# Retention attention with a SwiGLU block on one core: VectorE's operations on the shared port wait for GpSimd's, as GpSimd's already wait for VectorE's

## The chip, the cores and the metric

The kernel runs on one core of one Trainium2 chip, in one launch. The metric is the device time of that launch in microseconds (us); lower is better. The core's engines are TensorE (PE in the rows; PEld is its weight load), VectorE (DVE), ScalarE (ACT), GpSimd (POOL) and SyncE (SP, whose sequencer SPq issues nearly all DMAs). Each engine runs its own list of instructions in order, and instructions of different engines are ordered by semaphores alone.

## The reference

The input is q, k, v of shape (4, 8, 768, 64) in float32, a decay per head, and three weights of a gated layer with 512 inputs and 1536 hidden columns.

```python
for b in range(nb):                      # blocks of 64 tokens
    intra = einsum('bhic,bhjc->bhij', qb, kb) * Dmask
    intra = einsum('bhij,bhjd->bhid', intra, vb)
    inter = einsum('bhid,bhde->bhie', qb * lam_pow, kv_state)
    out[:, :, sl] = intra + inter
    kv_state = lam_block * kv_state + einsum('bhsd,bhse->bhde', kb * rev_pow, vb)
...                                      # x = out as 3072 tokens x 512
xn = x / sqrt(mean(x * x, -1) + 1e-6) * rms_g
g, val = xn @ w_gate, xn @ w_val
result = (g * sigmoid(g) * val) @ w_out  # float32
```

## The kernel before, in words

Tokens go in 6 groups of 512 (index `m`), heads in 4 pairs (`p`), hidden columns in 12 blocks of 128 (`f`). The work of all stages is interleaved:

- **Retention** for a group and a pair (class `Pair`): score products into PSUM tiles `pa`; VectorE multiplies them by the decay mask (`decay_a`, L497, tile `a`); ScalarE decays k (L487); GpSimd multiplies q by the powers in place (`decay_q`, L501, tile `qkv`); VectorE carries the state (L523, L525); TensorE sums in `po` (`mix_chunks` L538, `mix_states` L549, which reads the decayed q). ScalarE squares the result and GpSimd or VectorE adds the squares (`add_squares`, L578, tile `sq`).
- **Norm** (`first_norm_steps`, `norm_steps`, class `Norm`): the mean (L608), GpSimd's power -0.5 (`root`, L612, tile `y`), its rests (L619), the spread by TensorE (`pr`), the scaled rows `xn` (L636).
- **Float32 as two float16 parts**: every operand of a large product is split in a high part (ScalarE, a copy) and a low part, the difference (`low`: L440 for weights, L644 for x, L663 for the sums `tx`, L729 for the weights' sums `ws`, L922 and L1013 for the hidden rows, L290 for the output weights). VectorE or GpSimd makes the low parts.
- **Weights** (class `Weights`) are first decoded (L209 on ScalarE, `convert` L216 and L219 on VectorE), their squares summed (L416), a power of two chosen as scale (L426, L430) and undone later (`undo`, L445, tile `cg`).
- **Products**: in the first 24 units (one unit is a group and a block `f`) the gate and value products are done plainly (L668, tiles `pg` and `pv`). From then on they take seven half-size products instead of eight (`strassen`, L779, tiles `pa` and `pb`), with operand sums that GpSimd (`whole`, L708, tile `r`) and VectorE (`sums`, L717 to L721, tile `ws`) prepare; VectorE adds the partial products (L837, L845) and forms the hidden values (`mul_sums`, L857, tile `sg`), which SyncE stores (L873). SyncE also loads the prepared weights `gv` (L740) and `gw` (L745). The output product follows (L938, L1050).

**What sets the order.** All of this is recorded as steps, each with an engine, a cost, a due time and what it reads and writes. A planner (`Plan.run`) lays the steps on model clocks and returns one list; the kernel then issues its instructions in that order, so each engine's own list is fixed. The table `SHIFTS` moves due times.

**The shared port.** The planner treats all of GpSimd's steps, and those VectorE steps whose function stands in the set `SHARED`, as users of one port that only one of the two engines holds at a time (`Plan.shared`, L1150 to L1152):

```python
def shared(self, i):
    eng, fn = self.steps[i][0], self.steps[i][3]
    return eng == "POOL" or eng == "DVE" and fn.__name__ in self.SHARED
...
if self.shared(i):                     # in ready(): not before the other engine is through
    t = max(t, held["DVE" if eng == "POOL" else "POOL"] - 0.13)
```

So in the plan each of the two waits for the other. When the steps are issued (the loop at the end of the kernel, from L1961), a GpSimd step gets a real semaphore wait for the last shared VectorE operation that the plan puts ahead of it. A shared VectorE step gets no such wait for the GpSimd step ahead of it: it waits for its data alone. Nothing else in the program depends on this wait; it is there for the port.

In `SHARED` are, among others, `low`, `sums`, `mul_sums` (L857), `convert`, `add_squares`, `scale` (L426), `undo` (L445) and `rest` (L619).

Of the kernel before, what the change touches and what calls it, by code (L numbers as in the profile page):

```python
# [22 lines left out]
def retention_swiglu_kernel(  # L23
# [11 lines left out]
    nc = tc.nc  # L35
# [1463 lines left out]
    def arrive_steps():  # L1499
        def arrive():  # L1500
            pass

        step("LD", 4.3, -9, arrive, w=["cs", "come"])
        times = [0.75, 1.3, 1.55, 1.35, 1.85, 1.3, 1.3, 1.3]
        for p in range(NP):
            for i, c in enumerate(("qK", "kv")):
                step("LD", times[2 * p + i], -9, arrive, w=["come", *[f"q0_{p}:{x}" for x in c]])
        step("LD", 3.05, -9, arrive, w=["come", "gv0"])

    def ramp_steps():  # L1510
        pm = []

        def largest_of_all():
            pm.append(scales())

        def make_scales():
            scales_of(pm[0])

        step("DVE", 0.13, -3.1, largest, r=["cs"], w=["gmax"])
        step("PE", 0.3, -3.1, largest_of_all, r=["gmax"], w=["pmax"], new=[("pmax", "g")])  # L1520
        step("DVE", 1.33, -2.35, make_scales, r=["pmax"], w=["gs"])
        for p in range(NP):
            for part in range(3):
                w = f"pw{p}" if part == 2 else f"mask{2 * p + part}"
                step("DVE", 0.38, -3.2 + 0.4 * p + 0.15 * (part == 2), powers, p, part, r=["cs"] + ["wv11"] * (part == 2), w=[w])
        ats = [-2.85, -2.3, -2.0, -1.75]
        pairs = [Pair(0, p) for p in range(NP)]
        for q, at in zip(pairs, ats):
            pair_scores(q, at)
            pair_sums(q, at + 0.4)  # L1530
            pair_mix(q, at + 0.5)
        first_norm_steps(0, -0.3, 0.05)
        for p, at in enumerate(ATTENTION_1):
            q = Pair(1, p)
            pair_scores(q, at)
            pair_sums(q, at + 0.5)
            pair_mix(q, at + 0.6)
        first_norm_steps(1, 5.0, 0.05)
        for f, at in enumerate(CONVERT):
            wt = Weights(f)  # L1540
            if wt.halves:
                for i in range(2):
                    halved_steps(wt, at + 0.2 * i, i)
            else:
                convert_steps(wt, at)
                split_steps(wt, at + 0.35)
# [196 lines left out]
    def load_steps():  # L1743
        queue = [(1, 0), (1, 1), (1, 2), 1, (1, 3), *range(2, NF)]
        queue += [(m, p) for m in range(2, NG) for p in range(NP)]
        for n, key in enumerate(queue):
            cost = 2.65 if n < 5 else 3.0 if n < 10 else 3.6
            lasts = (0.1, 0.1, 0.5, 0.4)[n] if n < 4 else 2.3
            if isinstance(key, tuple):
                m, p = key  # L1750
                if key == (3, 1):
                    step("LD", 0.0, -9, operand_tiles, new=[("tx0", "in"), ("tx1", "in")],
                         w=[f"{t}:{o}{i}" for t in ("tx0", "tx1") for o in "hl" for i in range(2)]
                         + [f"vals{i}:{j}" for i in range(2) for j in range(2)])
                name = f"q{m}_{p}"
                step("LD", cost, -9, load_qkv, m, p, w=[f"{name}:{c}" for c in "qKkv"], new=[(name, "in")], lasts=lasts)
            else:
                step("LD", cost, -9, load_gv, key, w=[f"gv{key}"], new=[(f"gv{key}", "in")], lasts=lasts)
# [123 lines left out]
    with tc.manual_schedule(  # L1882
        engines={
            mybir.EngineType.PE, mybir.EngineType.DVE, mybir.EngineType.Activation,
            mybir.EngineType.Pool, mybir.EngineType.SP,
        }
    ):
        hs = {u: Hidden(u, m, f) for u, (m, f) in enumerate(units)}
        columns = {u: [] for u in range(2 * NF)}
        arrive_steps()  # L1890
        load_steps()
        ramp_steps()
        out_weights = [out_weight_steps(j, at) for j, at in enumerate(OUT_W)]
        end = len(units)
        pair = None
        for u in range(end):
            for f in COLUMNS.get(u, []):
                columns[u + 1].append(column_steps(f, u - 0.7))
            if u == FACTORS:
                factor_steps(u)  # L1900
            for f in range(NF):
                if int(SUMS[f]) == u:
                    sum_steps(f, SUMS[f])
            h = hs[u]
            m, f = h.m, h.f
            if u < 2 * NF:
                classical(u, h, columns[u])
                n = u - (2 * NF - 8)
                if 0 <= n < NP:
                    q = Pair(2, n)  # L1910
                    pair_scores(q, u + 0.62)
                    pair_sums(q, u + 0.64)
                    if pair:
                        pair_mix(pair, u + 0.63)
                    pair = q
                elif n == NP:
                    pair_mix(pair, u + 0.63)
                elif n == NP + 1:
                    norm_steps(2, u, 0.11)
                if u == 2 * NF - 1:  # L1920
                    pair = Pair(3, 0)
                    pair_scores(pair, u + 0.62)
            else:
                strassen(u, h)
                p = (f + 1) // 2 % HALF
                following = m + 2 if f == NF - 1 else m + 1
                if f % 2 == 0 and pair:
                    pair_sums(pair, u + 0.12)
                    pair_mix(pair, u + 0.3)
                    pair = None  # L1930
                if f % 2 and p < NP and following < NG:
                    pair = Pair(following, p)
                    pair_scores(pair, u + 0.1)
                if f == 2 * NP - 1 and m + 1 < NG:
                    norm_steps(m + 1, u, 0.2)
        if PLAIN:
            step("ROOM", 0.0, START[0] - 3, early_room, new=[("early", "big0")], w=["early:"])
        for m in range(PLAIN):
            for j in range(HALF):
                block_steps(m, j, START[m] - 1.5 - 0.3 * (HALF - 1 - j), 0.1)  # L1940
            plain_rows_steps(m, START[m], PLAIN_LENGTH)
        for o, at in zip(out_weights, OUT_SUMS):
            out_sum_steps(o, at)
        for i in range(2):
            room_step(i, START[PLAIN] - 3)
        for m, at in enumerate(START):
            if m < PLAIN:
                continue
            for j in range(HALF):
                t = at - AHEAD[j]  # L1950
                if m == NG - 1:
                    t = units.index((NG - 1, 2 * j + 1)) + 0.5
                operand_steps(m, j, t, 0.1)
            rows_steps(m, at, LENGTH)
        for i, by in SHIFTS.items():
            eng, cost, at, *rest = plan.steps[i]
            plan.steps[i] = (eng, cost, at + by, *rest)
        order = plan.run()
        now, gaps = 1.5, True
        traced, ahead = nc.cur_bb.bb.instructions, None  # L1960
        for t, i in order:  # L1961
            eng, cost, _, fn, args, _, _, new, _ = plan.steps[i]
            begun = len(traced)
            if eng == "PE":
                if any(name.startswith("pb") for name, _ in new):
                    gaps = False
                idle = t - now
                if gaps and idle > 0.8:
                    busy(int((idle - 0.5) / 0.24))
                now = t + cost  # L1970
            fn(*args)
            if plan.shared(i):

                engine = mybir.EngineType.Pool if eng == "POOL" else mybir.EngineType.DVE
                mine = [x for x in traced[begun:] if x.engine == engine]
                if eng == "DVE":
                    ahead = mine[-1].name
                elif ahead:
                    tc.add_manual_dep(
                        mine[0], ahead,  # L1980
                        mybir.DependencyInfo(mybir.DependencyClass.Sync, mybir.DependencyReason.DATA),
                        reason="shared port",
                    )
                    ahead = None

# [63 lines left out]
```

## Time and profile before

| | us |
|---|---|
| median of 3 runs (lowest, highest) | 629.96 (629.2, 631.78) |
| the profiled execution, its own time | 629.99 |
| its span, first to last instruction | 628.2 |
| busy: PE / PEld | 622.2 / 479.3 |
| busy: DVE / ACT / POOL | 452.8 / 383.9 / 127.6 |
| GpSimd instructions | 113 |
| VectorE instructions | 886 |

Busy time is the union of an engine's instructions. A matmul's end is modelled, so that a busy TensorE can still lose time between starts; and an operation that stands at a port counts as busy. In a row of the timeline, a number in brackets is the engine's idle time just before the instruction and what ended it. Granted clock is the share of TensorE's full 2.4 GHz; it was 1.000 over the whole span.

### The profile page before, as it was taken

How to read it: one execution, taken by the hardware profiler on the slowest of the kernel's cores; microseconds unless marked ns; L12 is line 12 of the kernel's file. 1: busy time of each engine (PE TensorE's matmuls, PEld its weight loads, DVE VectorE, ACT ScalarE, POOL GpSimd, SP SyncE). 2: the span in 40 equal slices, each digit the busy share in tenths (PEclk: the TensorE clock that was granted, in tenths of full speed). 3: DMA queues.
4: the chain of work that ended last, by engine and by line, in shares of the span. 5: the costliest groups of instructions: out<-in, count | busy, mean ns of one | idle time of the engine just before them, and what ended most of it. 6: DMA issues, size and time to landing. Idle time of an engine off the chain costs nothing.

```text
span 628.2 us, 14174 instructions
## 1 busy us (share of the span) xinstructions
PE 622.2 (99%) x5665; PEld 479.3 (76%) x5665; DVE 452.8 (72%) x886; ACT 383.9 (61%) x724; POOL 127.6 (20%) x113
## 2 busy tenths in 40 slices
PE   9999999999999999999999999999999999999997
PEld 8864444455657777668888888888889888888886
DVE  6889888777787778788875789634874778546641
ACT  3779799986546764568764685534853564445531
POOL 3531201142825665410020110011000110000000
DMA  8899898888646788878878667744675667343401
GB/s 320 305 318 299 313 313 290 288 279 290 231 148 226 258 284 273 275 265 284 269 268 297 216 212 225 244 179 152 226 224 179 202 207 248 109 135 105 148 18 51
DMA packets 56033, 144.05 MB, mean 229 GB/s; under 512 B 5920, under 2 KB 18208, under 8 KB 54560
## 3 DMA queue, kind: packets, MB, share of 16 engines
q1 hardware_dynamic: 55824, 142.64, 67.3%
q8 instruction: 44, 0.72, 0.5%
q10 hardware_dynamic: 144, 0.52, 0.3%
q14 instruction: 21, 0.17, 0.1%
HBM read 106.96 MB, written 36.18 MB: 228 GB/s over the span
## 4 chain that ended last, share of the span: by engine, by line
PE 94%; DMA 2%; DVE 1%; ACT 1%; SPq 0%; issue 0%; POOL 0%; ACTq 0%; POOLq 0%
PE o L1050 20%; PE pa L779 20%; PE pb L779 15%; PE pv L668 9%; PE pg L668 9%; PE o L938 5%; PE pa L477 4%; PE po L538 3%; PE po L549 3%; DMA qkv<-in_qkv_dram 2%; PE o_own L1050 2%; PE pst L510 2%; PE pss L589 1%; PE unread L144 1%; PE pr L630 0%
## 5 line engine op out<-in xcount | busy, mean ns | idle before, releaser
L779 PEld LDWEIGHTS <-gw 128*128 128x128 f16 x1440 | 139.5, 98 | 21.9 <-issue 0.8
L1050 PE MATMUL o<-wo,late 128*128 128x256 f16 x1152 | 143.9, 273 | 0.5 <-ACT late L1061 0.5
L1050 PEld LDWEIGHTS <-late 128*128 128x128 f16 x1260 | 123.0, 98 | 15.1 <-issue 0.8
L668 PEld LDWEIGHTS <-w_half 128*128 128x128 f16 x576 | 53.9, 98 | 60.5 <-issue 1.5
L833 ACT COPY tx<-pa 128x256 f32<-128x256 f32 x96 | 35.3, 371 | 72.9 <-PE pa L779 55.5
L779 PE MATMUL pa<-tx,gw 128*128 128x256 f16 x576 | 77.4, 273 | 0.0
L668 PE MATMUL pv<-x,w_half 128*128 128x512 f16 x288 | 69.2, 379 | 0.2
L668 PE MATMUL pg<-x,w_half 128*128 128x512 f16 x288 | 66.8, 379 | 0.0
L837 DVE TENSOR_TENSOR tx<-pb,tx 128x256 f32<-128x256 f32 x96 | 40.0, 420 | 31.4 <-PE pb L779 29.1
L779 PEld LDWEIGHTS <-gv 128*128 128x128 f16 x576 | 56.0, 98 | 7.4 <-issue 0.2
L501 POOL TENSOR_TENSOR qkv<-qkv,pw 128x512 f32<-128x512 f32 x24 | 30.6, 1275 | 74.8 <-PE pa L477 66.5
L845 DVE TENSOR_TENSOR sg<-pb,sg 128x256 f32<-128x256 f32 x48 | 20.1, 422 | 35.4 <-ACT sg L841 30.7
L1013 DVE TENSOR_TENSOR late<-s,late 128x1024 f16<-128x1024 f32 x30 | 37.3, 1253 | 5.2 <-ACT late L1009 5.1
L708 POOL TENSOR_TENSOR r<-w_half 128x512 f32<-128x512 f16 x24 | 27.7, 1163 | 63.3 <-DVE w_half L440 25.5
L497 DVE TENSOR_TENSOR a<-pa,mask 128x512 f32<-128x512 f32 x48 | 31.4, 683 | 12.0 <-PE pa L477 8.5
L779 PE MATMUL pa<-x,gv 128*128 128x256 f16 x288 | 39.3, 273 | 0.0
L779 PE MATMUL pb<-x,gv 128*128 128x256 f16 x288 | 39.3, 273 | 0.0
L779 PE MATMUL pa<-x,gw 128*128 128x256 f16 x288 | 39.0, 273 | 0.0
L779 PE MATMUL pb<-tx,gw 128*128 128x256 f16 x288 | 39.0, 273 | 0.0
L779 PE MATMUL pb<-x,gw 128*128 128x256 f16 x288 | 38.7, 273 | 0.0
L938 PE MATMUL o<-wo,early 128*128 128x512 f16 x144 | 34.9, 379 | 0.0
L729 POOL TENSOR_TENSOR ws<-ws,ws 128x512 f16<-128x512 f32 x24 | 28.8, 1210 | 29.3 <-DVE en L325 15.3
(152 smaller groups left out, 1031.0 us busy)
## 6 DMA issues: line engine op xcount, KB each, us to landing
gw<-gw_kept SPq DMA_DIRECT2D x48, 640.0 KB, 4.8
qkv<-in_qkv_dram SPq DMA_DIRECT2D x47, 512.0 KB, 6.0
h<-h_kept SPq DMA_DIRECT2D x30, 512.0 KB, 4.1
h_kept<-sg SPq DMA_DIRECT2D x48, 256.0 KB, 3.4
gv<-gw_kept SPq DMA_DIRECT2D x48, 256.0 KB, 4.4
raw_gv<-in_weights_dram SPq DMA_DIRECT2D x11, 1024.0 KB, 7.2
raw_o<-in_weights_dram SPq DMA_DIRECT2D x24, 256.0 KB, 4.4
gw_kept<-ws SPq DMA_DIRECT2D x12, 512.0 KB, 4.2
```

The costliest lines, as they stand in the source:

```text
L477: nc.tensor.matmul(self.pa[j][:, c, :], self.kT[r, c, :], self.qT[r, c, :], start=True, stop=True,)
L497: nc.vector.tensor_mul(self.a[:, j], self.pa[j], decay)
L501: eng.tensor_mul(self.qT, self.qT, pw[:, p : p + 1, :].broadcast_to([P, GC, P]))
L668: nc.tensor.matmul(ps, w[:, kk, :], x[:, kk, :], start=i == kk == 0, stop=i == 2 and kk == NK - 1,)
L708: nc.gpsimd.tensor_add(self.r[:, i], w[:, 0], w[:, 1])
L729: eng.tensor_sub(self.to[:, c, 1], self.t[:, c], self.to[:, c, 0])
L779: nc.tensor.matmul(ps, w(ow, k), x(ox, k), start=first and i == k == 0, stop=i == 2 and k == 1, skip_group_check=True,)
L833: nc.scalar.copy(self.val_sums[:, self.half(t)], self.pa)
L837: nc.vector.tensor_add(v, self.pb, v)
L938: nc.tensor.matmul(self.banks[t], h[:, oh, t * P : (t + 1) * P], wo[:, j, 3 + 2 * k : 5 + 2 * k, ow], start=j == k == i == 0, stop=j == HA ...
L1013: eng.tensor_sub(lo, of, hi)
L1050: nc.tensor.matmul(bank[:, t], ops[:, oh, t * P : (t + 1) * P], w[:, ow], start=n in (1, 2, 5) and q == i == 0 and (t == 0 or bank is own) ...
```

## The change

`ahead` held the last shared VectorE operation, and only a GpSimd step took it up as a wait. It becomes a table with an entry for each of the two engines: a shared step of either one takes up the other's latest entry, waits for it, and leaves its own. `mine[0]` is the first instruction of the step, which gets the wait, and `mine[-1]` the last, which is waited for.

```diff
-        traced, ahead = nc.cur_bb.bb.instructions, None
+        traced, ahead = nc.cur_bb.bb.instructions, {}
+        engines = {"POOL": mybir.EngineType.Pool, "DVE": mybir.EngineType.DVE}
         for t, i in order:
...
             fn(*args)
             if plan.shared(i):
 
-                engine = mybir.EngineType.Pool if eng == "POOL" else mybir.EngineType.DVE
-                mine = [x for x in traced[begun:] if x.engine == engine]
-                if eng == "DVE":
-                    ahead = mine[-1].name
-                elif ahead:
+                name = "POOL" if eng == "POOL" else "DVE"
+                mine = [x for x in traced[begun:] if x.engine == engines[name]]
+                other = ahead.pop("DVE" if name == "POOL" else "POOL", None)
+                if other:
                     tc.add_manual_dep(
-                        mine[0], ahead,
+                        mine[0], other,
                         mybir.DependencyInfo(mybir.DependencyClass.Sync, mybir.DependencyReason.DATA),
                         reason="shared port",
                     )
-                    ahead = None
+                ahead[name] = mine[-1].name
```

No instruction is added, removed or moved on any engine: all five lists hold the same rows in the same order. What changes is who waits. 63 VectorE instructions now wait for a GpSimd operation for which neither they nor an earlier instruction of VectorE waited before; older waits that a new one covers fall away. GpSimd's waits for VectorE stay as they were.

VectorE's list at the place where the sums of one weight block are made (`ws` from `r`), with the scores of a pair (`a`), the hidden values of a unit (`sg`) and a block of hidden rows (`early`) behind them. Semaphores stand in brackets: Pool is GpSimd's, DVE VectorE's own, Activation ScalarE's, DMAHW a DMA's.

```order
-L717 TENSOR_TENSOR ws_2717<-r_2585 128x256
+L717 TENSOR_TENSOR ws_2717<-r_2585 128x256 [waits Pool_49]
 L718 TENSOR_TENSOR ws_2717<-r_2585 128x256
-L720 TENSOR_TENSOR ws_2717<-r_2585,ws_2717 128x256 [waits DVE_49]
+L720 TENSOR_TENSOR ws_2717<-r_2585,ws_2717 128x256 [waits Pool_49]
 L721 TENSOR_TENSOR ws_2717<-r_2585,ws_2717 128x256 [waits DVE_49]
 L497 TENSOR_TENSOR a_2_2751<-pa_2_0_2730,mask 128x512 [waits DVE_49,PE_49]
 L497 TENSOR_TENSOR a_2_2751<-pa_2_1_2731,mask 128x512 [waits PE_49]
-L857 SCALAR_TENSOR_TENSOR sg_1_2636<-tx_2210,cg,sg_1_2636 128x512 [waits Activation_49]
+L857 SCALAR_TENSOR_TENSOR sg_1_2636<-tx_2210,cg,sg_1_2636 128x512 [waits Activation_49,Pool_49]
```

Three of these six steps now stand behind a GpSimd operation: the first sums behind the squares' addition, the second sums behind a `whole` (L708), the hidden values behind `decay_q` (L501). The order is as it was.

VectorE's list at the first halved weight block (f = 1), where the scale of one half is made (`e`, `sc`) and the low part of the other is formed (`w_half`):

```order
 L219 SCALAR_TENSOR_TENSOR w_1_553<-raw_gv_509,w_1_553 128x512 [waits DVE_49]
-L426 TENSOR_SCALAR e_1_697<-pn_0_674 128x1 [waits PE_49]
+L426 TENSOR_SCALAR e_1_697<-pn_0_674 128x1 [waits PE_49,Pool_49]
 L430 TENSOR_SCALAR sc_698<-e_1_697 128x1 [waits DVE_49]
 L497 TENSOR_TENSOR a_3_708<-pa_3_0_685,mask 128x512 [waits PE_49]
 L497 TENSOR_TENSOR a_3_708<-pa_3_1_686,mask 128x512 [waits PE_49]
-L440 SCALAR_TENSOR_TENSOR w_half_95<-w_0_552,sc_698,w_half_95 128x512 [waits Activation_49]
+L440 SCALAR_TENSOR_TENSOR w_half_95<-w_0_552,sc_698,w_half_95 128x512 [waits Activation_49,Pool_49]
```

Here L426 stands behind an addition of squares on GpSimd (L578), which itself waits for the L219 just ahead of L426, and L440 behind a `decay_q` (L501).

## Rows read from the trace of the kernel before

**Rows 1.** The page: the span, and each engine's busy time with its share of the span and its instructions.

```profile
span 628.2 us, 14174 instructions
PE 622.2 (99%) x5665; PEld 479.3 (76%) x5665; DVE 452.8 (72%) x886; ACT 383.9 (61%) x724; POOL 127.6 (20%) x113
```

**Rows 2.** All of TensorE's waits that the trace lists: who waited for whom, us in total, how often, the longest.

```profile
PE unread L144 <- POOL ident masks.py:199: 1.5, 1, 1.5
PE pss L589 <- POOL sq L578: 0.5, 1, 0.5
PE o L1050 <- ACT late L1061: 0.5, 1, 0.5
```

**Rows 3.** A stretch of the span in which GpSimd works most: its length, then busy us (and instructions) of PE, PEld, DVE, ACT and POOL, the granted clock, the DMAs' share, GB/s.

```profile
200.00:240.00 40.00, 40.00 (x411) 30.96 (x409) 30.71 (x58) 25.06 (x49) 25.25 (x22) 1.00 0.83 275
```

**Rows 4.** Timeline, VectorE and GpSimd at single places: start us, us, engine, line, operation, out<-in, shapes. First an L857 with GpSimd idle, then a GpSimd operation and the VectorE operation that waits for it.

```profile
246.34 0.75 DVE L857 SCALAR_TENSOR_TENSOR sg<-tx,cg,sg 128x512 f32<-128x512 f32 x1
...
247.17 1.16 POOL L708 TENSOR_TENSOR r<-w_half 128x512 f32<-128x512 f16 x1 [0.92 <-DVE sg L857]
...
248.36 0.42 DVE L717 TENSOR_TENSOR ws<-r 128x256 f32<-128x256 f32 x1 [0.28 <-POOL r L708]
```

**Rows 5.** Timeline at 232 us: VectorE, then GpSimd, then TensorE.

```profile
232.14 1.66 DVE L857 SCALAR_TENSOR_TENSOR sg<-tx,cg,sg 128x512 f32<-128x512 f32 x1
...
234.06 2.06 DVE L922 TENSOR_TENSOR early<-h,early 128x1024 f16<-128x1024 f32 x1
236.04 0.41 DVE L837 TENSOR_TENSOR tx<-pb,tx 128x256 f32<-128x256 f32 x1
...
232.11 1.15 POOL L708 TENSOR_TENSOR r<-w_half 128x512 f32<-128x512 f16 x1
233.88 1.15 POOL L708 TENSOR_TENSOR r<-w_half 128x512 f32<-128x512 f16 x1 [0.63 <-DVE sg L857]
...
236.51 0.38 PE L779 MATMUL pb<-tx,gw 128*128 128x256 f16 x2
```

**Rows 6.** Timeline at 211 to 217 us: VectorE, then GpSimd, then TensorE's weight loads.

```profile
211.78 1.11 DVE L717 TENSOR_TENSOR ws<-r 128x256 f32<-128x256 f32 x1
...
213.25 0.42 DVE L720 TENSOR_TENSOR ws<-r,ws 128x256 f32<-128x256 f32 x1
213.71 1.26 DVE L721 TENSOR_TENSOR ws<-r,ws 128x256 f32<-128x256 f32 x1
...
211.34 1.27 POOL L578 TENSOR_TENSOR sq<-sq,sq 128x512 f32<-128x512 f32 x1 [3.45 <-DVE ws L721]
213.37 1.32 POOL L708 TENSOR_TENSOR r<-w_half 128x512 f32<-128x512 f16 x1 [0.76 <-DVE ws L718]
215.05 1.15 POOL L708 TENSOR_TENSOR r<-w_half 128x512 f32<-128x512 f16 x1 [0.36 <-DVE ws L721]
216.16 1.27 POOL L501 TENSOR_TENSOR qkv<-qkv,pw 128x512 f32<-128x512 f32 x1
...
217.49 0.19 PEld L549 LDWEIGHTS po<-qkv,state 64*64 64x64 f32 x4 [0.23 <-POOL qkv L501]
```

**Rows 7.** Timeline at 40 to 43 us: VectorE, GpSimd, ScalarE, TensorE's weight load and matmuls.

```profile
40.57 0.15 DVE L426 TENSOR_SCALAR e<-pn 128x1 int32<-128x1 int32 x1
...
40.82 1.27 POOL L578 TENSOR_TENSOR sq<-sq,sq 128x512 f32<-128x512 f32 x1 [4.38 <-DVE e L426]
...
41.95 0.71 ACT L436 ACTIVATE w_half<-w,sc 128x512 f16<-128x512 f32 x1
...
42.77 0.31 PEld L668 LDWEIGHTS <-w_half 128*128 128x128 f16 x2
...
42.34 1.02 PE L668 MATMUL pg<-x,w_half 128*128 128x512 f16 x4
```

**Rows 8.** Timeline at 60 to 65 us: VectorE, GpSimd, ScalarE, TensorE.

```profile
60.15 0.22 DVE L445 TENSOR_SCALAR cg<-e,cx 128x2 int32<-128x2 int32 x1
61.09 0.69 DVE L216 TENSOR_SCALAR w<-w 128x1024 int32<-128x1024 int32 x1 [0.72 <-ACT w L209]
...
60.32 1.50 POOL L612 TENSOR_TENSOR y<-ms,power 128x4 f32<-128x4 f32 x1 [11.38 <-DVE sc L430]
...
63.15 0.63 ACT L416 ACTIVATE junk<-w 128x512 bf16<-128x512 f32 x1 [0.29 <-DVE w L219]
...
64.44 0.18 ACT L416 ACTIVATION_READ_ACCUMULATOR junk<-w 128x1 f32 x1
...
64.68 0.16 PE L420 MATMUL pn<-ssq,ones_b 128*128 128x2 bf16 x1
```

**Rows 9.** Timeline, VectorE and GpSimd at 28 us and at 264 us.

```profile
28.56 0.73 DVE L440 SCALAR_TENSOR_TENSOR w_half<-w,sc,w_half 128x512 f16<-128x512 f32 x1
28.11 1.03 POOL L612 TENSOR_TENSOR y<-ms,power 128x4 f32<-128x4 f32 x1 [0.62 <-DVE w_half L440]
...
263.81 0.42 DVE L274 TENSOR_TENSOR t<-wo_again,t 128x256 f32<-128x256 f32 x1
264.27 1.74 DVE L275 TENSOR_TENSOR t<-wo_again,t 128x256 f32<-128x256 f32 x1
264.04 1.69 POOL L663 TENSOR_TENSOR tx<-xt,tx 128x768 f16<-128x768 f32 x1 [3.60 <-DVE t L270]
```

**Rows 10.** GpSimd's longest wait by total, in the form of Rows 2.

```profile
POOL qkv L501 <- PE pa L477: 66.5, 15, 13.1
```

## Prediction

> **What bounds the kernel now.** First the page, then TensorE's waits, then the timeline where GpSimd works. TensorE is busy 99% of the span, VectorE 72%, GpSimd 20% [rows 1]. Its listed waits come to 1.5 + 0.5 + 0.5 = 2.5 us [rows 2], and in the stretch with most GpSimd work it is busy 40.00 of 40.00 us at granted clock 1.00, its 2.4 GHz level [rows 3]. That it is not only busy but issuing at pace shows in four matmuls of 512 columns in 1.02 us [rows 7]: with 0.38 us for the last one, the three starts between are 0.21 us apart, and 512 columns at 2.4 GHz are 0.213. So nothing later can make up for a delay of TensorE, and what another engine gains is worth at most those 2.5 us. The question is how much of the delay that the change gives VectorE reaches TensorE.
>
> Next, what the port does by itself. An L857 takes 0.75 us alone [rows 4], but 1.66 where a `whole` on GpSimd has started 0.03 us before it: that one ends at 233.26, L857 at 233.80, 0.54 later [rows 5]. So the port already holds VectorE back, and the lost time is booked as busy. The other way round, an L708 that should take 1.15 takes 1.32 where VectorE's L720 has started first [rows 6].
>
> **The change part by part.** Order and instructions stay; 63 VectorE instructions get a wait. A wait that does end VectorE's idle time ends 0.03 us after GpSimd's instruction (247.17 + 1.16 to 248.36 [rows 4]). I sorted the 63 by where GpSimd's operation lies in this execution.
>
> - 14: it was long over. They cost nothing, as nothing is waited for.
> - 33: it runs, and VectorE stands at the port already. Now VectorE starts 0.03 after it and takes its full time: for L857, 0.03 + 0.75 = 0.78 instead of 0.54, so +0.23 us with rounding [rows 4, 5]. For an L717 (211.78 + 1.11 = 212.89, GpSimd through at 212.61, so 0.28 before; now 0.03 + 0.42 = 0.45) it is +0.17 [rows 4, 6]. 33 times some 0.18 is 6.0 us of VectorE's time.
> - 7: it runs, and VectorE ran beside it unhindered. The largest is the low part L440 at 28.56, which ended at 29.29 beside the power L612 of 28.11 to 29.14 [rows 9]: now 29.17 + 0.73 = 29.90, +0.61. The others only met its tail; all seven together 1.35 us.
> - 9: it had not begun. GpSimd waits for one VectorE operation, and before its sequencer has taken that up, VectorE is already in the next. The first of the nine is L426 at 40.57, ahead of L578 at 40.82 [rows 7]; the last is L274 at 263.81, ahead of L663 at 264.04 [rows 9]. Now GpSimd goes first, and VectorE loses a whole operation of it, 1.2 to 1.9 us: 12.8 us in all. In five of them, though, the VectorE operation behind was stopped at the port anyway and no longer is (L275: 1.74 us where its neighbour takes 0.42 [rows 9]); that returns 4.0. Net 8.8.
>
> Sum: 6.0 + 1.35 + 8.8 = 16.2 us of VectorE's time. Were all of it on the path the kernel would end at 646; were none, at 630. What reaches TensorE I worked out at four places.
>
> - *40 us* [rows 7]. L426 starts at 40.82 + 1.27 + 0.03 = 42.12 and ends at 42.27; the scale behind it, as long, at 42.45. ScalarE's L436, which began at 41.95 because ScalarE was occupied until then, now starts at 42.48 and ends at 43.19, 0.53 late. TensorE's weights from it were loaded at 42.77, now at 43.24 to 43.34, and the matmul of 42.98 (the fourth of that row) starts at 43.34: **+0.36**.
> - *60 us* [rows 8]. The power L612 takes 1.03 where VectorE leaves it alone [rows 9], so it ends at 61.35, and L445 at 61.38 + 0.22 = 61.60 instead of 60.37. The next, L216, had idle time ahead of it (0.72) and starts some 0.43 late, since VectorE's next operation, where it waits for nothing, starts some 0.08 before its predecessor's end (L837 after L922 [rows 5]). ScalarE's squares wait for what follows (0.29 <- L219) and end at 64.62; TensorE's L420 comes 0.06 later, so nothing is left to take up the delay: **+0.43**.
> - *211 us* [rows 6]. L717 ends 0.17 late; L718 and the `whole` that waits for it too, so that one runs 213.54 to 214.69 (1.15, unhindered). L720 runs 214.72 to 215.14, L721 ends at 215.60 instead of 214.97. The second `whole` waits for it (0.36 <- L721) and `decay_q` stands behind that on GpSimd: 217.43 becomes 218.06. TensorE waits for just this (0.23 <- POOL qkv L501): **+0.62**.
> - *232 us* [rows 5]. L857 ends +0.23, the next L708 (0.63 <- L857) runs 234.11 to 235.26. L922, stopped, ended at 236.12, 1.09 after GpSimd; L717 above came to 0.28 where it takes 0.42 alone, 0.14 less, so alone L922 takes some 1.23 and now runs 235.29 to 236.52, +0.40. L837 follows, and TensorE takes up that PSUM tile at 236.51, 0.06 after L837's end: **+0.40**.
>
> These four have 1.55 + 1.22 + 0.63 + 0.40 = 3.8 us of VectorE's delay and give TensorE 1.8: 0.47 us for each. For the rest I take an estimate. Of 16.2 - 3.8 = 12.4 us, 1.0 lies behind 280 us, where GpSimd has few operations left; I cost that at nothing, covered by VectorE's idle time. The other 11.4 would give 5.4 at the same rate and 0 if slack takes them. I take three quarters of the rate, 4.0 us: nearer to the four places, as they lie in the same stretches and a delay that finds the slack used up passes on whole. SyncE's queue is in this: stores of the hidden values wait for L857, and weight loads stand behind them.
>
> So 629.99 + 1.8 + 4.0 = 635.8, say **636.0 us**, against the profiled execution's own time, which is within 0.1 of the median of the runs.
>
> One rule of the Trainium skill bears on the sizes. Beside the power L612, the L440 of 28.56 ran its 0.73 us undisturbed [rows 9]. The page "SBUF — State Buffer", section "Who interferes with whom", has it that whoever issues first holds the shared pair for the whole instruction and that a VectorE instruction with two SBUF inputs contends with a GpSimd instruction that reads SBUF; by that, L440 would have been stopped until 29.14 anyhow and the new wait would cost 0.2, not 0.6, some 0.2 us of the sum. The row decides: this operation leaves the port to others in its middle.
>
> **The rivals.**
>
> *Slack takes it: no change that can be measured.* The port serializes already, and the wait only makes that visible. TensorE pays the four places and little else: 629.99 + 1.8 to 3.0, about 632. For it: 33 of 63 waits replace a stop of nearly the same length, and VectorE is free 28% of the span [rows 1]. Against: in three of the four places TensorE took its operand within 0.06 us, or waited for it. By the page of the Trainium skill named above the loser at the port blocks fully already, which speaks for this rival too.
>
> *Faster.* GpSimd no longer finds VectorE in its way: seven of its operations lose 2.1 us of stretch in all (1.50 to 1.03 at 60 us [rows 8, 9] and 1.32 to 1.15 at 213 us [rows 6] are two). Where TensorE waits for GpSimd directly (0.5 for L578 [rows 2], 0.23 for L501 [rows 6]), it would gain. It decides if VectorE's delays reach TensorE nowhere: 0.7 us less, 629.3; with everything that TensorE waits for, 627.5. Neither passes 0.5%.
>
> *Much slower.* A wait for GpSimd is also a wait for what GpSimd waits for. `decay_q` waits for TensorE up to 13.1 us at a time [rows 10]. If delays shift the engines so that VectorE comes to its wait while GpSimd still stands at such a place, all work behind it on VectorE stands too. In this execution none of the nine was more than 0.4 us ahead of GpSimd's start, so that takes a shift of about a us; four such stops of 2 us each on top give 644.
>
> *The change does nothing.* The waits might be dropped as already implied. They are not: both lists show them.
>
> **How the numbers follow.** A difference of 0.5%, 3.15 us, is about what a measurement of this kernel can tell from no change. The forecast (TensorE loses 3.2 to 10 us) has 0.78, slack takes it 0.13, much slower 0.06, faster 0.03 (of which a third would pass 0.5%). So slower by over 0.5%: 0.84; within: 0.15; faster: 0.01. The range for 8 in 10: from 632.3 (the four places and a tenth of the rest) to 640.5 (all 11.4 at the rate, and 3 us of first stops).
>
> **What would show it.** VectorE's busy time falls by some 20 us, to about 433, since nothing stands at the port: L857 has 0.75 in every row. Its idle time behind GpSimd becomes some 45. GpSimd's busy time falls to about 125.5. L445 near 60 us starts after L612, L720 near 213 after L708. TensorE's list of waits grows entries near 40, 64, 217 and 236 us, and its instructions behind 280 us run as before, shifted by one amount. I am wrong if that shift is under 3 us, or if VectorE shows single waits for GpSimd over 3 us.

## The result, and the profile after

The change takes 638.11 us in the median of 4 runs (636.39 to 638.34), against 630.87 of 4 runs of the kernel before beside them (629.2 to 632.12): a ratio of **1.0103, interval 1.0083 to 1.0122**, or some 6.5 us slower; the two medians lie 7.2 apart. The forecast of 636.0 was 6.0 above the execution that it started from. The execution profiled here took 636.39; it is the fastest of the four, and its span is 6.4 us longer than that of before.

The page's span and busy times, to be held against [rows 1]:

```profile
span 634.6 us, 14194 instructions
...
PE 625.0 (98%) x5665; PEld 479.4 (76%) x5665; DVE 434.6 (68%) x886; ACT 384.2 (61%) x724; POOL 125.7 (20%) x113
```

VectorE does the same 886 instructions and is busy 18.2 us less: what was booked as work was standing at the port. GpSimd gains its 1.9 us, too. Neither shortens anything: where VectorE stood, it now waits, by the list of its own waits (who waited for whom, us in total, times, the longest), of which I show two entries. All those for GpSimd come to some 49 us in 55 waits; before they were 4.5 in 5.

```profile
DVE y L619 <- POOL ws L729: 4.1, 3, 2.3
...
DVE t L274 <- POOL tx L663: 1.8, 1, 1.8
```

The second is a turn that VectorE used to win, and so are L426's wait for L578 (1.5) and L445's for the power L612 (1.1), whose rows stand below. TensorE's list, in the same form, has eight entries that [rows 2] don't have; three of them:

```profile
PE pb L779 <- DVE sg L845: 0.8, 2, 0.5
...
PE po L538 <- DVE a L497: 0.4, 2, 0.2
...
PE pg L668 <- DVE en L325: 0.4, 1, 0.4
```

All eight are short, 0.2 to 0.5 us each. Seven lead straight back to VectorE; the eighth, for ScalarE's squares at 160 us (0.3), leads to a store of `ws` behind which ScalarE stood. The idle time of TensorE grows by 3.6 us (634.6 - 625.0 against 628.2 - 622.2); the other 2.8 us stand in its busy time, with the same 5665 matmuls, so its delay is read from starts. Setting the starts of the same matmul in the two traces side by side tells how late TensorE is at each place: 0.40 us ahead of the place at 42.8 (times of before), 1.02 at 64.7, 1.56 at 132.7, 3.18 at 209.9, 4.07 at 217.5, 4.98 at 236.5, 6.23 at 267.0, and from 283.5 to the end between 6.3 and 6.4. It gets next to nothing back (0.12 us at 42 us, 0.06 at 59).

The four places that the prediction had worked out, in the timeline of after (start us, us, engine, line, operation, out<-in, shapes; idle time ahead and what ended it). At 41 us, against [rows 7]:

```profile
41.35 1.27 POOL L578 TENSOR_TENSOR sq<-sq,sq 128x512 f32<-128x512 f32 x1 [4.56 <-DVE w L219]
...
42.66 0.16 DVE L426 TENSOR_SCALAR e<-pn 128x1 int32<-128x1 int32 x1 [1.48 <-POOL sq L578]
...
43.04 0.72 ACT L436 ACTIVATE w_half<-w,sc 128x512 f16<-128x512 f32 x1 [1.04 <-DVE sc L430]
...
43.81 1.04 PE L668 MATMUL pg<-x,w_half 128*128 128x512 f16 x4 [0.25 <-ACT w_half L436]
```

The turn has changed hands: L426 starts 0.04 after the addition of squares, ScalarE now waits for VectorE, and TensorE for ScalarE. At 61 us, against [rows 8]:

```profile
60.93 1.02 POOL L612 TENSOR_TENSOR y<-ms,power 128x4 f32<-128x4 f32 x1 [11.34 <-DVE sc L430]
...
61.99 0.23 DVE L445 TENSOR_SCALAR cg<-e,cx 128x2 int32<-128x2 int32 x1 [1.14 <-POOL y L612]
62.13 0.69 DVE L216 TENSOR_SCALAR w<-w 128x1024 int32<-128x1024 int32 x1
...
65.70 0.16 PE L420 MATMUL pn<-ssq,ones_b 128*128 128x2 bf16 x1 [0.25 <-ACT junk L416]
```

The power is back at its 1.02 us, and L445 and L216 stand behind it. At 215 to 222 us, against [rows 6]:

```profile
214.75 1.28 POOL L578 TENSOR_TENSOR sq<-sq,sq 128x512 f32<-128x512 f32 x1 [3.32 <-DVE ws L721]
216.06 0.42 DVE L717 TENSOR_TENSOR ws<-r 128x256 f32<-128x256 f32 x1 [0.79 <-POOL sq L578]
...
216.97 1.15 POOL L708 TENSOR_TENSOR r<-w_half 128x512 f32<-128x512 f16 x1 [0.94 <-DVE ws L718]
218.15 0.43 DVE L720 TENSOR_TENSOR ws<-r,ws 128x256 f32<-128x256 f32 x1 [1.33 <-POOL r L708]
...
219.12 1.16 POOL L708 TENSOR_TENSOR r<-w_half 128x512 f32<-128x512 f16 x1 [1.00 <-DVE ws L721]
...
220.23 1.28 POOL L501 TENSOR_TENSOR qkv<-qkv,pw 128x512 f32<-128x512 f32 x1
...
221.57 0.63 PEld L549 LDWEIGHTS po<-qkv,state 64*64 64x64 f32 x12 [0.24 <-POOL qkv L501]
```

No operation is stretched any more (L717 had 1.11, L721 1.26), and yet `decay_q` starts 4.07 later than before, where L578 started 3.41 later. At 236 to 242 us, against [rows 5]:

```profile
235.56 2.26 POOL L708 TENSOR_TENSOR r<-w_half 128x512 f32<-128x512 f16 x2 [0.81 <-DVE sq L578]
...
237.86 0.75 DVE L857 SCALAR_TENSOR_TENSOR sg<-tx,cg,sg 128x512 f32<-128x512 f32 x1 [1.07 <-POOL r L708]
...
238.69 1.15 POOL L708 TENSOR_TENSOR r<-w_half 128x512 f32<-128x512 f16 x1 [0.86 <-DVE sg L857]
...
239.88 1.23 DVE L922 TENSOR_TENSOR early<-h,early 128x1024 f16<-128x1024 f32 x1 [0.93 <-POOL r L708]
241.02 0.42 DVE L837 TENSOR_TENSOR tx<-pb,tx 128x256 f32<-128x256 f32 x1
...
241.49 0.71 PE L779 MATMUL pb<-tx,gw 128*128 128x256 f16 x5 [0.25 <-DVE tx L837]
```

L857 ends 0.75 after its start, everywhere: its longest of 49 is 0.753. And the largest single turn that the prediction had not followed to TensorE, against [rows 9]:

```profile
270.31 1.64 POOL L663 TENSOR_TENSOR tx<-xt,tx 128x768 f16<-128x768 f32 x1 [3.78 <-DVE t L270]
...
271.99 0.42 DVE L274 TENSOR_TENSOR t<-wo_again,t 128x256 f32<-128x256 f32 x1 [1.82 <-POOL tx L663]
272.45 0.42 DVE L275 TENSOR_TENSOR t<-wo_again,t 128x256 f32<-128x256 f32 x1
...
273.26 0.81 PE L779 MATMUL pb<-x,gw 128*128 128x256 f16 x6 [0.45 <-DVE sg L845]
```

L274 starts 8.18 later than before, L275 ends 6.86 later, and L663 started 6.27 later: the turn takes 1.8 from L274, gives 1.3 back at L275, which no longer stands at the port, and leaves some 0.6 us. TensorE takes all of that (+0.61).

### The profile page after: what moved, and what is told of

Read it like the earlier page. It is cut to its first block, busy times and chain, and to the rows that moved or that the text cites. A ratio compares the mean times of both kernels' runs of the same rounds, so it can differ in the third digit from the quotient of the medians.

```text
span 634.6 us, 14194 instructions
## 1 busy us (share of the span) xinstructions
PE 625.0 (98%) x5665; PEld 479.4 (76%) x5665; DVE 434.6 (68%) x886; ACT 384.2 (61%) x724; POOL 125.7 (20%) x113
## 4 chain that ended last, share of the span: by engine, by line
PE 60%; POOL 6%; DVE 6%; DMA 4%; issue 2%; ACT 1%; SPq 1%; POOLq 0%; ACTq 0%; DVEq 0%
PE o L1050 20%; PE pa L779 17%; PE pb L779 13%; PE o L938 2%; POOL ws L729 2%; PE o_own L1050 2%; POOL r L708 2%; PE pa L477 2%; DMA gw_kept<-ws 1%; PE pg L668 1%; DMA qkv<-in_qkv_dram 1%; PE po L538 1%; PE po L549 1%; POOL qkv L501 1%; DVE early L922 1%
## 5 line engine op out<-in xcount | busy, mean ns | idle before, releaser
L837 DVE TENSOR_TENSOR tx<-pb,tx 128x256 f32<-128x256 f32 x96 | 40.0, 420 | 27.1 <-PE pb L779 23.5
L501 POOL TENSOR_TENSOR qkv<-qkv,pw 128x512 f32<-128x512 f32 x24 | 30.7, 1278 | 75.0 <-PE pa L477 61.1
L845 DVE TENSOR_TENSOR sg<-pb,sg 128x256 f32<-128x256 f32 x48 | 20.1, 422 | 34.4 <-ACT sg L841 30.3
L708 POOL TENSOR_TENSOR r<-w_half 128x512 f32<-128x512 f16 x24 | 27.5, 1157 | 65.1 <-DVE w_half L440 25.9
L849 ACT ACTIVATE sg<-sg,cg 128x256 f32<-128x256 f32 x48 | 24.2, 507 | 17.8 <-DVE sg L845 17.5
```

Of the source, the lines that this page charges most:

```text
L501: eng.tensor_mul(self.qT, self.qT, pw[:, p : p + 1, :].broadcast_to([P, GC, P]))
L708: nc.gpsimd.tensor_add(self.r[:, i], w[:, 0], w[:, 1])
L837: nc.vector.tensor_add(v, self.pb, v)
L845: nc.vector.tensor_add(g, self.pb, g)
L849: nc.scalar.activation(self.sg[:, half], self.sg[:, half] if t else self.pa, AF.Silu, scale=cg[:, self.f, 0:1],)
```

## The experiments

Theory: the new waits of both kinds cost. The nine turns, in which GpSimd now goes first, and the 54 others, at most of which VectorE stood at the port anyway, each delay VectorE, and in the first 280 us a part of each delay reaches TensorE, which gives nothing back. Rivals: the turns alone make the loss, and the 54 are free; or the other way round. Each edit is one of the loop that adds the waits. `TURNS` and `LATE` are numbers of the plan's steps.

**1. Without the nine turns.** GpSimd's waits and VectorE's 54 others stay.

```diff
+        TURNS = {231, 277, 413, 433, 441, 655, 786, 1126, 2164}
...
-                if other:
+                if other and (name == "POOL" or i not in TURNS):
```

> The change without the nine waits at which VectorE ran ahead of a GpSimd operation that had not begun; the other 54 stay. Theory (delay travels along the queues and only what finds no slack reaches TensorE; small delays add up with large ones): TensorE loses part of what the change costs, 1.5 to 3 us, so about 632.3 where the kernel before takes 630. Rival A (the nine turns are the whole cost): 0 to 0.5 us. Rival B (every wait costs the same, as a wait itself is what is dear): 54/63 of 6.4 us, 5.5 us. In the trace: the step of TensorE at 64.7 us is gone, that at 216 to 218 us is smaller, and no VectorE operation is longer than alone except those behind the nine places.

634.04 us (633.54 to 634.78, 6 runs) against 631.19 of 13 runs of before: 1.0043, interval 1.0029 to 1.0057, +2.7 us. At 61 us its timeline has the old order again:

```profile
61.40 0.22 DVE L445 TENSOR_SCALAR cg<-e,cx 128x2 int32<-128x2 int32 x1
61.57 1.51 POOL L612 TENSOR_TENSOR y<-ms,power 128x4 f32<-128x4 f32 x1 [11.35 <-DVE sc L430]
62.35 0.69 DVE L216 TENSOR_SCALAR w<-w 128x1024 int32<-128x1024 int32 x1 [0.73 <-ACT w L209]
```

L445 is ahead of the power, which is stretched again. TensorE's steps at 42.8 and 267 us are gone, at 64.7 it even gets 0.22 back, that at 216 to 217.5 is 0.21 instead of 0.89; those at 132.7 (+0.54) and 236.5 (+0.37) are all there. So the 54 waits do cost 2.7 us, though by the prediction's sorting 33 of them take the place of a stop of nearly the same length and 14 come when GpSimd is long through. This run doesn't part the 33 from the 7 that now stop an operation which ran unhindered; but 216 and 236.5 us are places where VectorE stood at the port before [rows 5, 6], and TensorE loses 0.21 and 0.37 there.

**2. The nine turns alone.**

```diff
-                if other:
+                if other and (name == "POOL" or i in TURNS):
```

> Only the nine waits at which VectorE ran ahead of a GpSimd operation that had not begun; the other 54 are left out. Theory: 2 to 3.2 us slower than the kernel before (the 8.8 us of VectorE's net delay at some 0.3), and together with the other half less than the 6.4 us of the whole change, since a delay that finds the slack used up passes on whole. Rival A (the nine are the whole cost): 6 us. Rival B (all waits alike): 0.9 us. In the trace: TensorE steps at 42.8 us (0.2 to 0.5), 64.7 us (0.4) and 217 us (about 1), VectorE's stops at the port stay (L857 at 232 us takes 1.66 us).

633.35 us (631.2 to 636.25, 8 runs), 1.0040, interval 1.0023 to 1.0057, +2.5 us. The pattern is the complement of the first. Two rows of its timeline:

```profile
42.78 1.04 PE L668 MATMUL pg<-x,w_half 128*128 128x512 f16 x4 [0.25 <-ACT w_half L436]
...
64.40 0.16 PE L420 MATMUL pn<-ssq,ones_b 128*128 128x2 bf16 x1 [0.25 <-ACT junk L416]
```

TensorE has steps at 42.8 (+0.43), 64.7 (+0.19), 216.6 to 217.5 (+0.46) and 267 us (+0.44), and none at 132.7 and 236.5. Those at 64.7 and 217 are half of what was expected (0.4 and about 1). This execution is the fastest of the eight: from 28 to 300 us its TensorE loses 1.2 us, so the trace accounts for only a part of the median's 2.5. Both rivals fall. The two parts make 2.7 + 2.5 = 5.2 us, the whole 6.0 to 6.5. The ratios' intervals (each some 0.2% wide to a side for the whole, 0.15% for the parts) don't tell 5.2 from 6.5, so the times leave open whether the parts make each other worse.

The traces show that they do, in the executions traced. At 172.4, 179.6, 204.4, 209.9 and 243.6 us TensorE has steps of 0.31, 0.26, 0.26, 0.35 and 0.20, together 1.4 us, in the change; in the fifth and the sixth run they are the same within 0.02, and neither part has any of them. The matmul of 209.9 in the change, in the first experiment and in the second:

```profile
213.08 0.81 PE L779 MATMUL pb<-x,gw 128*128 128x256 f16 x6 [0.30 <-DVE sg L845]
...
211.67 0.83 PE L779 MATMUL pb<-x,gw 128*128 128x256 f16 x6
...
209.60 0.83 PE L779 MATMUL pb<-x,gw 128*128 128x256 f16 x6
```

The L845 that it waits for is later against TensorE than before by 0.59 us in the change, by 0.03 and 0.00 in the parts. What slack takes up from one part alone passes on when both are there.

**3. The eleven waits behind 280 us alone.** The prediction had costed them at nothing.

```diff
-                if other:
+                if other and (name == "POOL" or i in LATE):
```

> Only the waits behind 279 us. Theory: VectorE's idle time there takes them, TensorE is late by under 0.1 us at the end. Rival B (all waits alike): 11 of 63, 1.1 us. Rival C (a slower clock or transfers, not the waits before 280 us, make the end late): more than 1 us.

One run: 631.86 us, among the 13 of before (630.24 to 632.61). VectorE has the waits, 7.8 us in 11 with the old ones, and the time doesn't show them. A single run would not show half a us either. In its trace TensorE falls back by 0.8 us behind 280 us, where under 0.1 was expected. Of this 0.48 lies at 332 us, where the eighth run, without these waits, has 0.38, and 0.26 at 455 us, behind an L857 whose wait no GpSimd operation ended. In the change itself it is 0.17. So the trace ties no loss to the eleven waits; that they cost nothing is not shown closer than this.

**4. No port waits at all.** GpSimd's old waits for VectorE go too.

```diff
-                if other:
+                if False:
```

> No wait for the port in either direction: GpSimd does not wait for VectorE's shared operations, VectorE not for GpSimd's. Theory (who goes first at the port is what costs, not the semaphore): GpSimd comes first at more places than before, VectorE stands at the port there, and the kernel is 2 to 4 us slower than the kernel before; VectorE's busy time grows by some 3 us and GpSimd's by 3 to 4. Rival D (waits for the port only cost, as the port serializes by itself): the same as before or up to 0.7 us faster.

637.43 us (635.38 to 638.98, 6 runs), 1.0092, interval 1.0073 to 1.0112, +5.8 us: right in direction, larger than expected. VectorE's busy time is 462.9 us, 10 more than before where some 3 were expected, GpSimd's 133.0, 5.4 more. Its timeline at 214 to 220 us:

```profile
214.23 2.45 POOL L708 TENSOR_TENSOR r<-w_half 128x512 f32<-128x512 f16 x2 [0.43 <-DVE ws L721]
214.68 0.99 DVE L717 TENSOR_TENSOR ws<-r 128x256 f32<-128x256 f32 x1
215.59 1.38 DVE L718 TENSOR_TENSOR ws<-r 128x256 f32<-128x256 f32 x1
216.65 1.44 POOL L501 TENSOR_TENSOR qkv<-qkv,pw 128x512 f32<-128x512 f32 x1
217.00 1.37 DVE L720 TENSOR_TENSOR ws<-r,ws 128x256 f32<-128x256 f32 x1
...
219.68 0.43 PE L538 MATMUL po<-a,qkv 128*64 128x128 f32 x2 [1.25 <-DVE a L497]
```

With nothing to hold GpSimd back, three of its operations follow one another, and VectorE gets between them with one operation each: three that take 0.42 alone take 0.99, 1.38 and 1.37. TensorE waits 1.25 us for the scores behind them. So the waits that the kernel had before are worth their 5.8 us, and at this place what they do is give VectorE the turn.

**5. The change again**, beside the next three, on another chip.

> The change itself, on the same chip as the runs beside it. Theory: 6.4 us slower than the kernel before, as first measured, and more than the two parts measured apart (2.7 us without the nine turns, 2.5 us with the nine alone, 5.2 us together), since a delay that finds the slack used up passes on whole. Rival (the parts simply add): 5.2 us.

637.49 us (635.84 to 638.91, 6 runs) against 631.51 of 11 runs of before: 1.0094, interval 1.0074 to 1.0113. TensorE's steps are at the same places with the same sizes (42.8: +0.43, 132.7: +0.53, 216.4 to 217.5: +0.88, 236.5: +0.37, 267: +0.61). The interval, 4.7 to 7.1 us, holds both the 6.4 expected and the 5.2 of two parts that simply add; the five steps that neither part has are here again.

**6. No port wait for the power.** `root` (L612) leaves no entry in the table, so VectorE may run beside L612 as before.

```diff
-                ahead[name] = mine[-1].name
+                if fn.__name__ != "root":
+                    ahead[name] = mine[-1].name
```

> The change without the waits for the power L612 on GpSimd (L440 near 28.6 us and L445 near 60.2 us lose theirs). Theory (this operation leaves the port to others in its middle, so that only the wait stops VectorE): L440 runs its 0.73 us beside L612 again, L445 ends before it, TensorE's step at 64.7 us is gone, and the kernel is 0.3 to 1 us faster than the whole change, 5.4 to 6.1 us over the kernel before. Rival (the port is held for the whole instruction): L440 stands at the port until L612's end and little is gained there.

637.89 us (636.01 to 639.57, 6 runs), 1.0097, interval 1.0076 to 1.0118: not faster than the change beside it, where 0.3 to 1 us were expected. That is a miss. Its timeline at 29 and at 61 us does what was meant:

```profile
29.01 1.03 POOL L612 TENSOR_TENSOR y<-ms,power 128x4 f32<-128x4 f32 x1 [1.01 <-DVE w_half L440]
29.45 0.74 DVE L440 SCALAR_TENSOR_TENSOR w_half<-w,sc,w_half 128x512 f16<-128x512 f32 x1
...
61.28 0.22 DVE L445 TENSOR_SCALAR cg<-e,cx 128x2 int32<-128x2 int32 x1
61.45 1.51 POOL L612 TENSOR_TENSOR y<-ms,power 128x4 f32<-128x4 f32 x1 [11.34 <-DVE sc L430]
```

TensorE's step at 64.7 us is gone. But in this execution those at 160 us (0.72 instead of 0.23 in the fifth run's trace) and at 260 us (1.03 instead of 0.26) are larger. What they are larger by comes from stores of this execution, not from VectorE's earlier start. SyncE issues the store of `ws` (L732) at 254.94 here and at 255.01 in the fifth run, yet ScalarE's L725, which overwrites `ws`, can start only at 262.17 against 260.72. GpSimd's L729 waits for it, VectorE's L857 for L729 by the added wait (1.82 us, in the fifth run 1.05), and TensorE for VectorE:

```profile
262.17 1.04 ACT L725 CAST ws<-ws 128x1024 f16<-128x1024 f32 x1 [1.41 <-DMA gw_kept<-ws]
...
265.60 0.75 DVE L857 SCALAR_TENSOR_TENSOR sg<-tx,cg,sg 128x512 f32<-128x512 f32 x1 [1.82 <-POOL ws L729]
...
267.34 0.81 PE L779 MATMUL pb<-tx,gw 128*128 128x256 f16 x6 [0.87 <-DVE tx L837]
```

At 160 us, too, L725 starts 5.20 us after the issue of its store, in the fifth run 4.72. A place that is mended by 0.2 us is not seen beside that in one trace, and six runs don't show it in the median.

**7. Only VectorE waits.** GpSimd's waits for VectorE go, VectorE's for GpSimd come.

```diff
-                if other:
+                if other and name == "DVE":
```

> The mirror of the kernel before: VectorE waits for GpSimd's operations, GpSimd does not wait for VectorE's. Theory (what costs is VectorE coming second; GpSimd now comes first at more places than before): 4 to 8 us slower than the kernel before, with GpSimd's busy time some 6 us longer, as it now stands at the port instead. Rival E (one direction of waits is as good as the other, two are too many): within 1 us of the kernel before.

640.16 us (639.28 to 642.7, 4 runs), 1.0142, interval 1.0118 to 1.0166, +9 us, a little above the 4 to 8 expected; GpSimd's busy time grew by 3.3 us, not by 6. Its page and one entry of its TensorE waits:

```profile
PE 625.8 (98%) x5665; PEld 479.8 (75%) x5665; DVE 463.4 (73%) x886; ACT 383.5 (60%) x724; POOL 130.9 (21%) x113
```

```profile
PE po L538 <- DVE a L497: 1.4, 2, 1.2
```

VectorE is as busy as without any wait (462.9): GpSimd, unheld, catches it in operations that no wait covers, as in the fourth run, and the same 1.2 us wait of TensorE is there. With the fourth and fifth run this makes a table of two by two, as ratios to before:

| | VectorE doesn't wait | VectorE waits |
|---|---|---|
| GpSimd waits | 1 | 1.0094 (1.0074 to 1.0113) |
| GpSimd doesn't | 1.0092 (1.0073 to 1.0112) | 1.0142 (1.0118 to 1.0166) |

GpSimd's waits gain in either column, VectorE's cost in either row. It is not order at the port that pays, but, as far as the rows of the fourth run at 214 us show it, that VectorE is first there.

**8. One wait alone**, that of L445 for the power near 60 us.

```diff
-                if other:
+                if other and (name == "POOL" or i == 277):
```

> The kernel before with one of the 63 waits, that of L445 near 60.2 us for the power L612. Theory: L445 starts 0.03 us after L612's end, L612 takes 1.02 us instead of 1.50, and TensorE's L420 near 64.7 us comes 0.2 to 0.43 us later than in the kernel before, against the matmuls just before it; the whole time is the same as before within what a run shows.

One run, 632.08 us, read for its trace. At 60 to 65 us:

```profile
60.02 1.02 POOL L612 TENSOR_TENSOR y<-ms,power 128x4 f32<-128x4 f32 x1 [11.17 <-DVE sc L430]
61.08 0.23 DVE L445 TENSOR_SCALAR cg<-e,cx 128x2 int32<-128x2 int32 x1 [1.14 <-POOL y L612]
...
64.78 0.16 PE L420 MATMUL pn<-ssq,ones_b 128*128 128x2 bf16 x1 [0.25 <-ACT junk L416]
```

TensorE has one step here, +0.19 over the stretch from 59 to 65 us (it waits 0.25 at L420, and had gained 0.06 at 59.3), and none in the neighbourhood. This wait by itself costs TensorE 0.19 us, not the 0.43 of the prediction; the mechanism is shown, its size was off.

## Why the prediction was right, point by point

**What bounds the kernel: right.** TensorE's loss, added up by places, is 6.4 us, and so is the span's. GpSimd's 1.9 us and VectorE's 18.2 us of shorter busy time bought nothing. The median, 638.11, is 2.1 above the forecast of 636.0; 0.9 of that is that the kernel before took 630.87 beside it, not the 629.96 that was known.

**VectorE's own balance: right as far as the trace shows it.** Forecast were busy 433, idle behind GpSimd 45, GpSimd busy 125.5; they are 434.6, 49.0 and 125.7. That 33 of the waits only take the place of a stop, at +0.17 to +0.23 each, shows at L857 near 232 us: it ends 4.81 later where the `whole` ahead of it starts 4.57 later, +0.24. The first experiment shows at 216 and 236.5 us that such waits are not free in time.

**The four places.** Forecast +0.36, +0.43, +0.62 and +0.40, together 1.81; measured +0.43, +0.19, +0.89 and +0.37, together 1.88. The sum is right because two errors cancel.

- *40 us*: the mechanism as told. L578 was itself 0.53 late where TensorE was 0.40 late. TensorE started 0.05 after ScalarE's end, not 0.15 as reckoned, which takes back most of that; 0.07 over is left.
- *60 us*: mis-sized, the term "so nothing is left to take up the delay: +0.43". The prediction let L612 be as late as TensorE, but it started only 0.61 later than before where TensorE was 0.83 late: 0.43 − 0.22 = 0.21. In the eighth experiment, whose VectorE has no new wait up to here, L612 also starts 0.2 sooner against TensorE than before (0.30 earlier, TensorE 0.09). So VectorE had that slack in these executions and not in the one that the prediction read. The row cited for a power that VectorE leaves alone [rows 9] has L440 running in it; that the power takes 1.02 beside an idle VectorE shows only after the change, at 60.93.
- *211 us*: between L578 and L501 the delay grows by 4.07 − 3.41 = 0.66, the forecast's 0.62. The other 0.23 (3.41 − 3.18) had come about on VectorE before this place, ahead of the L721 for which L578 waits, and TensorE had not met it yet. Here a delay that waited on VectorE was handed over whole at the next place where TensorE waited.
- *232 us*: L837 ends 4.99 later where the `whole` at 232 starts 4.57 later, +0.42; TensorE's step is +0.37.

**The rest, estimated at 4.0: measured 4.5.** 6.4 − 1.9 = 4.5 lies at places that were not worked out, 132.7 us (+0.54), 160 (+0.36), 172 (+0.31), 179 (+0.25), 204 (+0.26), 210 (+0.36), 231 (+0.28), 260 (+0.27) and 267 (+0.61) before all; that at 160 hangs on a store's landing as well, and is +0.23 in the fifth run. One rate for all kinds was good enough: the nine turns gave 2.5 us for a forecast of 8.8 us of VectorE's time, the others 2.7 for 7.4, that is 0.28 and 0.37. The reason given, that a delay which finds the slack used up passes on whole, is borne out by the five steps that only both parts together have. That three quarters of the rate came so near is in part luck: it was a choice between all and nothing, and no row gave it. **Behind 280 us** nothing was forecast, and +0.17 came.

**The rivals.** *Slack takes it* falls with the ratio's interval, whose lower end is 5.2 us above before. *Much slower*: no wait of VectorE for GpSimd is over 2.3 us, none is the stop behind `decay_q` that it needs. Its mechanism, a wait for what GpSimd waits for, is there in small at 260 us of the sixth run (0.77 us). *Faster*: where TensorE waits for GpSimd's L578, at 21 us, it waits 0.52 us as before (0.53), and L501 at 217 us comes 4.07 later, not earlier, though it runs undisturbed. *The change does nothing* falls with 55 waits.

**The rule weighed there.** The page "SBUF — State Buffer" of the Trainium skill, section "Who interferes with whom", would have L440 stopped by the power until the power's end. In the sixth experiment, where the wait is away, L440 starts at 29.45, inside the power's 29.01 to 30.04, and takes 0.74; in [rows 9] it took 0.73. The measurement decides against the rule for this operation. Yet the 0.3 to 1 us expected from leaving that wait away did not show in the time.

## What to carry to other kernels

Two engines that share a port already take turns; a semaphore did not make that cheaper here, it only made it visible, and it cost some 0.2 us of VectorE's time a turn. What a wait there can buy is a choice of who goes first: let the engine go first whose results the bound engine needs, and let only the other one wait. A wait for an engine is also a wait for all that this engine waits for, a late store included. Before taking "the engine is busy less" for a gain, look whether the busy time was standing at a port, and add up the bound engine's small new waits place by place.

## What the runs showed of the hardware

- An operation that stands at the port counts as busy and is through sooner than one that waits for a semaphore: L857 ended 0.54 us after the GpSimd operation that stopped it [rows 5], and ends 0.78 after it with a wait (0.03 + 0.75); for L717 it is 0.28 [rows 6] against 0.45.
- Where GpSimd waits by a semaphore for one VectorE operation and the next one on VectorE waits for nothing, VectorE's next can be first, as at the nine turns. GpSimd's L708 starts 0.08 us after the L857 ahead of it has ended (238.69 after 238.61), and VectorE's next operation, without a wait, starts ahead of its predecessor's end (62.13 where L445 ends at 62.22).
- The power (128x4) and L440 (128x512, from 29.45 to 30.19 beside 29.01 to 30.04) leave each other alone: 0.74 and 1.03 us. With L216 (128x1024, int32) in its second half it takes 1.51 and ends 0.04 after L216 (63.08 after 63.04, first experiment). Which property of the two VectorE operations decides, no run here shows.
- Two executions of one kernel differ by some us at places without new waits: in the fifth run TensorE was 0.5 us late at 6.3 us already, in the first execution of the same kernel it was not. In the eighth, TensorE waits 1.41 us at 536 us for a DMA (`gw<-gw_kept`), far behind the one wait that was added. Differences of 0.3 us in the whole are not to be read from one trace; those at one place, where the rows on both sides agree, are.
